# Making the lower halves of the weights' words on ScalarE instead of GpSimd in an attention and Mish feed-forward kernel

## The chip, the core and the metric

The kernel runs on one core of one Trainium2 chip. The metric is the device time of one execution in microseconds; the kernel before was timed three times, and the median counts. A profiled execution of the same program gives the trace.

The core's engines are TensorE (PE in the profile, with its weight loads as PEld), VectorE (DVE), ScalarE (ACT), GpSimd (POOL) and SyncE (SP), which here issues the transfers. Each takes its instructions in the order in which the program lists them for it.

## The reference, cut to what matters

Attention with two kinds of local masks (8 batches, 8 heads, 576 positions, head size 64) is followed by a feed-forward layer with a Mish gate; all in float32:

```python
attn_out = _attn_ref(q, k, v)                      # windowed softmax attention
x = attn_out.transpose(0, 2, 1, 3).reshape(4608, 512)
h = x @ w_in                                       # 512 x 2048
sp = where(h > 20.0, h, log1p(exp(minimum(h, 20.0))))
g = h * tanh(sp)
out = g @ w_out                                    # 2048 x 512
```

The weights w_in and w_out come as arrays of 64-bit words. The host shows the kernel each word as two 32-bit halves, and the kernel makes of the lower half a number from 0 to 7 by a multiplication, an addition and a rounding to int32, which it then puts beneath bits of the upper half.

## The kernel before, in words

The tokens are cut into 16 units of 288 (`u` = 0 to 15, two to a batch). For each unit the kernel loads q, k and v, makes scores, exponentials and values, transposes the result into `x`, multiplies it by w_in (`ff1`, line 790), evicts it through Mish on ScalarE (line 796), forms a gate `g` as two float16 halves, and multiplies by w_out (`ff2`, line 972, in the first three units; `product`, line 933, after).

The weights are read once, ahead of and among the first units. Each of w_in (`k` = 0) and w_out (`k` = 1) is taken in four column groups `g` and two parts `p`, and each part goes through these steps, named `wl`, `wm`, `ww`, `ws` and `wp` with `k.g.p` behind them:

- `wl`: SyncE issues two transfers of 512 KB (line 348 for w_in, line 350 for w_out) into one of four buffers `raw`; group 1 of w_in goes straight to `w2`. A buffer is free again when the `wp` of an earlier part has read it.
- `wm`: the upper halves are scaled into the place of the weights (line 370 on ScalarE for w_in, line 368 on GpSimd for w_out).
- `ww`: three steps. The first makes the lower halves in place (line 411, on GpSimd); the second and third join the bits on VectorE (lines 413 and 415). Part 0.3.0 goes through them in two pieces, so line 411 runs 17 times.
- `ws`: TensorE takes a maximum's ingredient over the joined words (lines 382 and 385), and VectorE makes a scale of it.
- `wp`: the words are split into two float16 halves, on ScalarE (line 422) and VectorE (line 424).

There is no planner at run time: a list `ORDER`, written out in the kernel, names every step, and each time that a name occurs, one more piece of that step (up to its next `yield`) is issued. The instructions of one engine run in the order of the list, and an instruction that waits keeps all that stand behind it on its engine. A number after `=` gives the PSUM bank, of which there are four. The two places of the list that the prediction speaks of most are these (0.2.0's first `ww` is in the first line, 1.2.0's in the last but one):

```python
ff0.7=0 wp0.1.1 ff0.0=1 ww0.2.0 ff0.0 fs0.3 ww0.1.0 ff0.1=2 lv2 ff0.7 ww0.2.1 wp0.1.1 wp0.1.0 ww0.2.1 wl1.1.0 fs0.1
wp0.1.0 ff0.0 pr1 ff0.1 lv2 ff0.7 ff0.6 ff0.1 va1.2=1 wm0.2.0 pr1 va1.2 va1.0=0 va1.0 ld2 va1.0 pr1=3 ld2 ff0.2=2
...
ld3 wl1.2.0 ww1.0.1 ff1.2 ff1.0 ww1.2.0 ff1.6 ff1.7 ww1.0.0 ff1.1=1 ww1.1.0 gt0.1 wp1.1.0 ld3 ff1.5=3 xa2 ff1.1
ff1.1 ww1.0.0 ww1.0.1 tp2.0=2 wp1.1.0 wl1.2.1 tp2.0 ws1.0=1 gt0.2 ws1.0 ff1.5 wp1.0.0 tp2.1=2 ww1.0.1 ff1.2 wp1.0.0
```

An `ff` step has three pieces: two groups of 12 matmuls on TensorE, and the eviction through Mish on ScalarE (`hm`, line 796), which frees the bank. `fs` are small scales on ScalarE (line 769), `va` the values' matmuls (line 689), `sp` the scores' matmuls (line 577, which read `knd`), `tx` the transposes into x (lines 738, 744 and 746), `lv` the loads of v, with a small memset on GpSimd (line 489) ahead of the first of them (line 501).

Of the kernel before, what the change touches and what calls it, by code (L numbers as in the profile page):

```python
# [14 lines left out]
U32 = mybir.dt.uint32  # L15
I64 = mybir.dt.int64
AF = mybir.ActivationFunctionType
ALU = mybir.AluOpType
# [11 lines left out]
LOW_SCALE, LOW_BIAS = 0.9375 * 2.0 ** -29, -2.0 ** -5  # L30
# [157 lines left out]
def attn_mish_ffn_kernel(  # L188
# [11 lines left out]
    nc = tc.nc  # L200
# [154 lines left out]
    def w_dst(k, g, p):  # L355
        c = slice(p * WIDE, (p + 1) * WIDE)
        return w1[g][:, c] if k == 0 else w2[:, g, c]

    def pieces(k, g, p):
        return [slice(c, c + 1) for c in range(WIDE)] if (k, g, p) in BY_BLOCK else [slice(0, WIDE)]  # L360
# [45 lines left out]
    def w_words(k, g, p):  # L406

        lo, hi = raws[k, g, p]
        a = w_dst(k, g, p).rearrange("p c a n -> p c (a n)").bitcast(I32)
        for c in pieces(k, g, p):  # L410
            nc.gpsimd.tensor_scalar(lo[:, c], lo[:, c].bitcast(U32), LOW_SCALE, LOW_BIAS, ALU.mult, ALU.add)
            yield
            nc.vector.scalar_tensor_tensor(a[:, c], a[:, c], 3, lo[:, c], ALU.logical_shift_left, ALU.bitwise_or)
            yield
            nc.vector.scalar_tensor_tensor(lo[:, c], hi[:, c], -0x80000000, a[:, c], ALU.bitwise_and, ALU.bitwise_or)
            yield
# [585 lines left out]
    def keep_warm_short(n):  # L1002
        keep_warm(n, ones_b)


    STEPS = {"ld": loads, "qp": spread_q, "lv": loads_v, "pr": prep, "sp": scores_of_kind, "sc": scores, "tp": transpose_p, "va": values, "tx": transpose_x,
             "ex": exps, "wl": w_load, "wm": w_max, "ws": w_scale, "ww": w_words, "wp": w_split, "fs": ff_scales,
             "ff": ff1, "gt": gate, "fo": ff2, "kw": keep_warm, "kh": keep_warm_short, "ft": top_scale, "rs": rescale,
             "su": w_sums, "so": sums_open, "gq": gate_of, "ga": gate_sums, "fq": product, "mf": masks_first, "cs": constants, "xa": x_alloc, "ol": open_late, "mr": masks_late}
# [52 lines left out]
```

## Time and profile before

| what | us |
|---|---|
| three runs | 858.32, 859.57, 861.2; median 859.57 |
| the profiled execution, its own time | 862.81 |
| span of the profiled execution | 860.9 |
| TensorE busy | 842.1 (98%) |
| VectorE, ScalarE, GpSimd busy | 636.1 (74%), 477.8 (55%), 96.0 (11%) |
| mean granted TensorE clock | 0.992 of full speed |

The span runs from the first to the last instruction that the trace records; 1.9 us of the execution lie around it. Busy time is summed over instructions of an engine. The weights' steps end by 142 us; after that the list holds none of them.

### The profile page before, as it was taken

Reading aid. Unit: us, or ns where it says so; the run is one execution under the profiler, and the core shown is the slowest. Engines: PE = TensorE matmul, PEld = TensorE weight load, DVE = VectorE, ACT = ScalarE, POOL = GpSimd, SP = SyncE. Lnnn points to the kernel's source line nnn. Section 1 sums busy time; section 2 is a strip of 40 time slices with the busy share of each in tenths; the row PEclk is TensorE's granted clock in tenths of the full one; section 3 lists DMA queues with packets and bytes.
Section 4 is the critical chain, followed back from the end, with each engine's and each line's share of the span. In section 5 each row is a group of like instructions: output and inputs, shape, how many; then the busy total and the mean of one; then the engine's idle time right before and its main releaser. Section 6 shows DMA issues by size and latency. Waiting matters only on the chain.

```text
span 860.9 us, 32197 instructions
## 1 busy us (share of the span) xinstructions
PE 842.1 (98%) x14818; PEld 727.3 (84%) x14821; DVE 636.1 (74%) x818; ACT 477.8 (55%) x615; POOL 96.0 (11%) x99
## 2 busy tenths in 40 slices
PE   8798999999999999999999999999999999999998
PEld 7486777788788998988999889988889889988898
DVE  3788998586999897968777587977878764854353
ACT  2464655453486558765753775766446656624342
POOL 5116583210010001000000000010000000000000
PEclk9989999999999999999999999999999999999999
DMA  8648543366320437253623373725335160421001
GB/s 270 213 151 266 154 146 87 73 144 130 70 57 13 126 80 178 57 144 96 126 67 102 69 150 76 131 72 102 94 73 109 43 127 18 57 40 34 1 22 37
DMA packets 154887, 86.29 MB, mean 100 GB/s; under 512 B 92288, under 2 KB 150656, under 8 KB 154752
## 3 DMA queue, kind: packets, MB, share of 16 engines
q1 hardware_dynamic: 154752, 84.24, 40.9%
q8 instruction: 116, 1.90, 1.0%
q14 instruction: 19, 0.16, 0.1%
HBM read 56.89 MB, written 9.44 MB: 77 GB/s over the span
## 4 chain that ended last, share of the span: by engine, by line
PE 86%; DMA 7%; DVE 3%; SPq 2%; ACT 1%; issue 1%; POOL 0%; DVEq 0%; POOLq 0%; ACTq 0%
PE b L790 40%; PE b L933 31%; PE b L972 8%; DMA vf<-in_vd 4%; PE b L689 4%; PE b L577 3%; DMA raw<-in_w_in 2%; DMA knd<-in_kdT 1%; DVE g L903 1%; SPq L348 1%; DVE hm L909 0%; DVE w L424 0%; SPq L501 0%; PE b L385 0%; ACT g L901 0%
## 5 line engine op out<-in xcount | busy, mean ns | idle before, releaser
L790 PE MATMUL b<-x,w 128*128 128x288 f16 x3072 | 393.4, 286 | 0.2 <-ACT hm L796 0.2
L790 PEld LDWEIGHTS <-w 128*128 128x128 f16 x3072 | 295.4, 98 | 75.5 <-issue 0.6
L903 DVE SCALAR_TENSOR_TENSOR g<-hm,sg,g 128x1152 f16<-128x1152 f32 (+1 forms) x104 | 131.3, 1272 | 53.7 <-ACT g L901 52.9
L933 PE MATMUL b<-g,w 128*128 128x144 f16 x2496 | 164.9, 226 | 0.8 <-issue 0.7
L933 PEld LDWEIGHTS <-w 128*128 128x128 f16 x2496 | 158.4, 98 | 3.2 <-issue 1.1
L796 ACT ACTIVATE hm<-b,fs 128x576 f32<-128x576 f32 x128 | 92.8, 738 | 113.5 <-PE b L790 99.2
L901 ACT ACTIVATE g<-hm,sg 128x1152 f16<-128x1152 f32 (+1 forms) x104 | 116.0, 1127 | 40.1 <-PE b L933 26.4
L481 POOL COPY qp<-qn 128x576 f32<-128x576 f32 x15 | 34.9, 2326 | 433.6 <-DMA qn<-in_qT 317.9
L909 DVE TENSOR_TENSOR hm<-hm 128x576 f32<-128x576 f32 x104 | 79.0, 763 | 1.9 <-ACT hm L796 0.4
L972 PE MATMUL b<-g,w 128*128 128x288 f16 x576 | 73.3, 286 | 0.1
L947 ACT ACTIVATE y<-b,fo 128x288 f32<-128x288 f32 x52 | 40.6, 786 | 58.9 <-PE b L933 57.6
L972 PEld LDWEIGHTS <-w 128*128 128x128 f16 x576 | 55.6, 98 | 14.4 <-DVE w L424 0.3
L952 DVE SCALAR_TENSOR_TENSOR y<-b,fo,y 128x144 f32<-128x144 f32 x78 | 33.6, 478 | 45.8 <-PE b L933 22.7
L933 PE MATMUL b<-g,g 128*128 128x144 f16 x936 | 66.6, 226 | 0.3 <-DVE y L952 0.2
L933 PE MATMUL b<-g,late_sums 128*128 128x144 f16 x936 | 65.9, 226 | 0.0
L933 PEld LDWEIGHTS <-g 128*128 128x128 f16 x936 | 60.6, 98 | 2.2 <-issue 0.6
L933 PEld LDWEIGHTS <-late_sums 128*128 128x128 f16 x936 | 60.0, 98 | 0.5
L727 ACT CAST x<-xs 96x512 f16<-96x512 f32 (+1 forms) x39 | 26.7, 686 | 30.9 <-DMA x<-x 17.1
L729 DVE TENSOR_TENSOR x<-xs,x 96x512 f16<-96x512 f32 (+1 forms) x39 | 30.1, 772 | 16.6 <-ACT x L727 16.4
L545 DVE SCALAR_TENSOR_TENSOR vh<-vn,s,vh 128x2688 f16<-128x2688 f32 (+1 forms) x13 | 35.2, 2705 | 8.6 <-ACT vh L543 8.6
L705 DVE TENSOR_TENSOR xs<-b,rec 96x512 f32<-96x512 f32 (+1 forms) x48 | 37.2, 776 | 4.4 <-DVE rec L703 0.5
L689 PEld LDWEIGHTS <-pT 64*32 64x32 f16 (+1 forms) x3276 | 30.2, 90 | 5.3 <-issue 3.6
(127 smaller groups left out, 821.1 us busy)
## 6 DMA issues: line engine op xcount, KB each, us to landing
qn<-in_qT SPq DMA_DIRECT2D x15, 576.0 KB, 5.3
vn<-in_vd SPq DMA_DIRECT2D x66, 128.0 KB, 3.8
raw<-in_w_out SPq DMA_DIRECT2D x16, 512.0 KB, 5.2
out_T<-y SPq DMA_DIRECT2D x26, 288.0 KB, 2.8
raw<-in_w_in SPq DMA_DIRECT2D x12, 512.0 KB, 7.4
vn<-in_v SPq DMA_DIRECT2D x14, 288.0 KB, 4.2
knd<-in_kdT SPq DMA_DIRECT2D x14, 224.0 KB, 4.7
vn<-in_v SPq DMA_DIRECT2D x12, 256.0 KB, 3.7
```

What stands on the lines that cost most here:

```text
L481: nc.gpsimd.tensor_copy(qp.rearrange("p (b r i) -> p b r i", r=NR, i=SQ // NR), d["q"][:, :2 * HT].rearrange("p (b i r) -> p b r i", r=NR, ...
L545: nc.vector.scalar_tensor_tensor(lo, src, s, hi, ALU.mult, ALU.subtract)
L689: nc.tensor.matmul(avv[s * SQ:(s + 1) * SQ, a, t - t0, h * (D + 1):(h + 1) * (D + 1)], p, vv[vi][ks, v0:v0 + D + 1], start=(i == 0), stop= ...
L705: nc.vector.tensor_tensor(xs.rearrange("p (a t h e) -> p a t h e", a=2, h=2, e=D), avv[:, :, :, 1:AW - 1].rearrange("p a t (h e) -> p a t ...
L790: nc.tensor.matmul(ph[:, h, :HT], w1[j][:, c, wi, k * P:(k + 1) * P], x_of(d, xi, c), start=(n == 0), stop=(n == len(seq) - 1))
L796: nc.scalar.activation(d["m"][p][:, half, k0:k0 + 2], ph[:, :, :HT], AF.Mish, scale=d["fs"][:, j:j + 1])
L901: nc.scalar.activation(hi, src, AF.Identity, scale=sg)
L903: nc.vector.scalar_tensor_tensor(lo, src, sg, hi, ALU.mult, ALU.subtract)
L909: nc.vector.tensor_tensor(a, a, b, op=op)
L933: nc.tensor.matmul(acc[e], left(l, e, p, wi)[:, k * P:(k + 1) * P], right(gi, k), start=(n in opens and p == 0 and q == 0), stop=(last and ...
L947: nc.scalar.activation(into(half, t), by(acc), AF.Identity, scale=fo)
L972: nc.tensor.matmul(po[:, :HT], w2[:, e, j, wi, k * P:(k + 1) * P], d["g"][j][:, gi, k, :], start=(j == 0 and n == 0), stop=(j == NCH - 1 a ...
```

## The change

The first `ww` step becomes a ScalarE instruction that computes the same multiplication, addition and rounding, with the same operands and at the same places of the list. GpSimd loses 17 instructions, ScalarE gains 17. All else stays.

```diff
         lo, hi = raws[k, g, p]
         a = w_dst(k, g, p).rearrange("p c a n -> p c (a n)").bitcast(I32)
         for c in pieces(k, g, p):
-            nc.gpsimd.tensor_scalar(lo[:, c], lo[:, c].bitcast(U32), LOW_SCALE, LOW_BIAS, ALU.mult, ALU.add)
+            nc.scalar.activation(lo[:, c], lo[:, c].bitcast(U32), AF.Copy, scale=LOW_SCALE, bias=LOW_BIAS)
             yield
             nc.vector.scalar_tensor_tensor(a[:, c], a[:, c], 3, lo[:, c], ALU.logical_shift_left, ALU.bitwise_or)
             yield
```

## Rows read from the trace of the kernel before

**Rows 1.** The page's busy times of the engines, over the span

```profile
PE 842.1 (98%) x14818; PEld 727.3 (84%) x14821; DVE 636.1 (74%) x818; ACT 477.8 (55%) x615; POOL 96.0 (11%) x99
```

**Rows 2.** Sum of windows from 140 to 860 us, busy time by engine

```profile
sum 720.00, PE 715.92 PEld 627.45 DVE 526.31 ACT 406.82 POOL 28.66; mean PE 19.89 PEld 17.43 DVE 14.62 ACT 11.30 POOL 0.80
```

**Rows 3.** TensorE's waits: line, releaser, total us, times, longest

```profile
PE b L577 <- DMA knd<-in_kdT: 1.8, 2, 1.4
...
PE b L382 <- DVE w L413: 0.9, 1, 0.9
PE b L577 <- DVE x L746: 0.8, 1, 0.8
...
PE b L385 <- DVE w L413: 0.7, 1, 0.7
```

**Rows 4.** Line 411: duration ns min/median/max, and its longest idle's end

```profile
L411 POOL TENSOR_SCALAR raw<-raw x15: 639/1139/1685, 8.3 to 124.8; 128x1024 int32<-128x1024 uint32 x13, 128x512 int32<-128x512 uint32 x2
...
  DMA raw<-in_w_in: 16.4, 4
```

**Rows 5.** ScalarE by line and form, to 140 us: busy, mean ns, idle before

```profile
L422 ACT ACTIVATE w<-raw,ws 128x1024 f16<-128x1024 f32 x14 | 17.3, 1243 | 9.2 <-DVE ws L394 3.7 <-PE b L659 3.6 <-DVE ws L401 1.2
...
L370 ACT ACTIVATE w<-raw 128x1024 f32<-128x1024 f32 x5 | 5.7, 1131 | 17.4 <-DMA raw<-in_w_in 17.4
```

**Rows 6.** ScalarE's timeline around part 0.1.1: start us, us, instruction, idle before

```profile
48.08 0.64 ACT L744 CAST x<-b 128x576 f16<-128x576 f32 x1 [0.41 <-PE b L738]
```

**Rows 7.** ScalarE's timeline around the place of 0.2.0

```profile
57.96 0.30 ACT L769 ACTIVATE fs<-f,f 128x1 f32<-128x1 f32 x1
...
60.87 2.63 ACT L796 ACTIVATE hm<-b,fs 128x576 f32<-128x576 f32 x4
65.42 1.14 ACT L370 ACTIVATE w<-raw 128x1024 f32<-128x1024 f32 x1 [1.92 <-DMA raw<-in_w_in]
```

**Rows 8.** SyncE's timeline, transfers of 0.2.0 and 1.2.0

```profile
59.61 1.08 SPq L348 DMA_DIRECT2D raw<-in_w_in  x2
...
94.47 1.03 SPq L350 DMA_DIRECT2D raw<-in_w_out  x2
```

**Rows 9.** SyncE's waits from 66 to 130 us: total, times, longest

```profile
SPq L501 <- POOL vf L489: 4.2, 1, 4.2
```

**Rows 10.** TensorE's timeline behind the place of 0.2.0

```profile
62.51 1.34 PEld L689 LDWEIGHTS b<-vf,pp 64*32 64x32 f32 x120 [0.24 <-ACT hm L796]
...
77.66 6.97 PE L790 MATMUL b<-x,w 128*128 128x288 f16 x48
```

**Rows 11.** Half-microsecond windows of TensorE: length, busy, granted clock, DMA share, GB/s

```profile
42.00:42.50 0.50, 0.00 (x0) 0.51 0.47 137
42.50:43.00 0.50, 0.02 (x3) 0.50 0.25 73
...
48.50:49.00 0.50, 0.50 (x7) 0.66 0.10 30
...
76.00:76.50 0.50, 0.50 (x56) 0.65 0.89 291
...
79.50:80.00 0.50, 0.50 (x6) 0.94 1.04 315
```

**Rows 12.** Timeline around the place of 1.2.0, four engines

```profile
92.50 1.94 DVE L424 SCALAR_TENSOR_TENSOR w<-raw,ws,w 128x1024 f16<-128x1024 f32 x1 [1.35 <-ACT w L422]
...
98.47 2.00 ACT L796 ACTIVATE hm<-b,fs 128x576 f32<-128x576 f32 x3
99.26 4.57 PE L790 MATMUL b<-x,w 128*128 128x288 f16 x36 [0.22 <-ACT hm L796]
...
102.44 1.50 POOL L411 TENSOR_SCALAR raw<-raw 128x1024 int32<-128x1024 uint32 x1 [9.06 <-DMA raw<-in_w_out]
```

**Rows 13.** VectorE's line 413 beside one of line 411, and undisturbed

```profile
22.71 1.90 DVE L413 SCALAR_TENSOR_TENSOR w<-w,raw 128x1024 int32<-128x1024 int32 x1
...
26.28 1.21 DVE L413 SCALAR_TENSOR_TENSOR w<-w,raw 128x1024 int32<-128x1024 int32 x1
```

## The prediction

> **What bounds the kernel now.** I began with the page's busy times. TensorE works for 842.1 of 860.9 us [rows 1]; the reader should see that it is the bound over the whole, and that a lighter GpSimd (96.0 us) can't matter by its load. The next view is the windows by stage. From 140 us to 860 us TensorE is busy for 715.92 of 720 us [rows 2], so 842.1 - 715.9 = 126.2 us of its work and nearly all its idle time (14 us) lie in the first 140 us, and the weights' steps lie there too. Whatever the first 140 us lose is not won back afterwards: only 4 us of idle time are left there.
>
> The third view is TensorE's waits [rows 3]. Those that bear on the change are 0.9 us and 0.7 us for VectorE's line 413 (the joining of the words), 1.8 us for the transfer of `knd`, and 0.8 us for VectorE's line 746. Then comes line 411 itself [rows 4]. Its instructions last 1.14 us in the middle, and what they mostly wait for is a transfer. That is the point of this case: on GpSimd such a wait costs little, since hardly anything stands behind it. On ScalarE the evictions of the banks stand behind it. So the last views are the timelines of ScalarE, SyncE and TensorE around each place.
>
> **The change, part by part.** *The price of the work.* ScalarE has no instruction of this shape in the trace with an unsigned input and an int32 output. The nearest rows have the same 128x1024 elements and read the same words with a stride: line 370 at 1.131 us, line 422 at 1.243 us [rows 5]. I take 1.13 (both multiply by a constant), with 1.24 as the other end. Seventeen of these are at most 19 us more on ScalarE, which is busy for 477.8 of 860.9 us [rows 1]; the load alone makes no bound. I see no loading of a function table for it: the two lines of rows 5 stand in the same stretch between Exp and Mish without one.
>
> *Fifteen of the seventeen places.* At the places of groups 0.3 and 0.0 ScalarE and GpSimd wait for the same transfer, and ScalarE is ready for it; TensorE is multiplying ones to stay warm there. The pieces of w_out but for 1.2.0 come to a ScalarE whose data has landed, or to one that waits for TensorE anyway. Part 0.1.1 stands between two evictions of `x`, where ScalarE idles 0.41 us ahead of the second [rows 6], which takes up part of the piece; what is left can make the first `ff` late. For all fifteen I take 0.2 us, between 0 and 1.1 us (one piece quite uncovered).
>
> *Place A, part 0.2.0.* In the list its piece stands behind `wp0.1.1` and ahead of `fs0.3`, `wp0.1.0`, `fs0.1` and the four Mish evictions of ff0.0, ff0.7, ff0.6 and ff0.1, and the data is not there yet. SyncE issues the transfer at 59.61 [rows 8], and ScalarE's own line 370 for the same part, which stands behind the evictions, starts at 65.42 when the transfer ends its wait [rows 7]. Now ScalarE waits at this point from about 59 us on, with all four evictions behind it. It goes on at 65.42 + 1.13 = 66.55. From `fs0.3` to the first eviction took 60.87 - 57.96 = 2.91 us, and an eviction takes 2.63 / 4 = 0.66 [rows 7], so bank 1 is free at 66.55 + 2.91 + 0.66 = 70.1. TensorE's next work, `va1.2`, takes bank 1, and started at 62.51 right behind that eviction [rows 10]. The wait is 70.1 - 62.5 = 7.6 us.
>
> What is late next is shortened by this. Between 62.5 and 84.6 TensorE waited 0.9 us for line 413 of this same part, and 1.8 us for `knd` [rows 3]; both are ready when TensorE comes later, so 2.7 us come back. The clock is the other thing. After TensorE's wait that ends just before 43.0, the granted clock is at 0.51, that is 1.2 GHz, from 42.0 until it rises between 48.5 and 49.0 [rows 11]: some 5.6 us of work at half speed behind a wait. After the wait for `knd` it is low from 76.0 to about 79.5 [rows 11]. The new wait is longer than either, so I put 5.6 us of low clock behind it. Streamed matmuls lose half of that, 2.8 us; but the first 2 us are short float32 matmuls of 65 columns, which lose less: 2.3 us, bounds 1.8 and 2.8. The low stretch behind the `knd` wait goes away: 3.5 us, of which 1.84 us are the streamed matmuls from 77.66 on [rows 10], so 0.9 to 1.7 us come back, I take 1.3. Place A: 7.6 - 2.7 + 2.3 - 1.3 = 5.9 us, bounds 5.0 and 6.8.
>
> A gain lies in the same place. SyncE's line 501 waits 4.2 us for GpSimd's memset [rows 9], which stood behind the waiting line 411. GpSimd no longer waits, so SyncE issues what follows (among it `knd`) 4.2 us sooner. But TensorE is late by then, so it is worth nothing beyond the 1.8 us counted above.
>
> *Place B, part 1.2.0.* Its piece stands between the eviction of ff1.0 and those of ff1.6 and ff1.7. The three evictions ran together from 98.47, while GpSimd's line 411 waited 9.06 us for its transfer, till 102.44 [rows 12]. On ScalarE it ends at 102.44 + 1.13, and the eviction of ff1.6, which frees bank 3, at 104.2. TensorE comes to ff1.5, which takes bank 3, after 12 of the 36 matmuls that start at 99.26 in 4.57 us: 99.26 + 1.52 = 100.8 [rows 12]. If place A moves both alike, the wait is 3.4 us. It does so as far as I can follow: SyncE issued this transfer at 94.47 [rows 8], right after VectorE's line 424 ended, 92.50 + 1.94 = 94.44 [rows 12], which frees its buffer, and this hangs on ScalarE's and TensorE's late work. Another low stretch follows a wait of this length; on streamed matmuls with a few transposes I take 2.3 us again (1.8 to 2.8). Place B: 5.7 us. Its bounds are 0, where the transfer lands 3.4 us sooner against TensorE than before, and 7.5, where it lands over a microsecond later.
>
> *What comes back behind it.* The waits of 0.7 us for line 413 and 0.8 us for line 746 [rows 3] lie at 117 and 138 us, where TensorE will be late and VectorE less disturbed. I take 1.0 of the 1.5 us, bounds 0 and 1.5.
>
> *A relief for VectorE.* Line 413 took 1.90 us where a line 411 ran beside it, and 1.21 us alone [rows 13]. The Trainium skill, page "SBUF — State Buffer", section "SBUF: two separate sides", says that VectorE instructions with two SBUF inputs and GpSimd instructions that read SBUF take one port pair in turn, the later one waiting for the other's whole length; the 0.69 us of these rows agrees with that. By that rule the change speeds VectorE at up to 17 places. As a mechanism of this kernel it can shorten only TensorE's waits for VectorE: 0.9 + 0.8 + 0.7 = 2.4 us [rows 3].
>
> *The sum.* 0.2 + 5.9 + 5.7 - 1.0 = 10.8 us. The profiled execution took 862.81 us of its own (its span and 1.9 us around it), so one like it would take 873.6. It stands 3.2 us above the median of the runs, 859.57, on which the sum gives 870.4. I predict 870.
>
> **The rivals.** *Only place A costs.* For it: SyncE is 4.2 us ahead at 63 us, and GpSimd's lighter load can bring 1.2.0's transfer forward against TensorE. Against it: the buffer's release at 94.44 is what the issue waited for. 859.6 + 0.2 + 5.9 - 1.0 = 864.7.
>
> *ScalarE stays behind.* After place B eight or so late pieces could each press on an eviction, at 1.13 us and a further low stretch: 4 to 8 us more, 874 to 878. Against it: ScalarE has waits of its own for TensorE in that stretch.
>
> *No change.* The relief of VectorE is all that counts, because the evictions prove not to wait: 859.6 - 2.4 = 857.2, just inside the 0.3% (2.6 us) that measurement of this kernel can tell from none. The skill's rule above is what speaks for it. Against it is the order of ScalarE's queue.
>
> *Faster.* SyncE's 4.2 us bring `knd` in time, and with the wait of 1.8 us its low clock of 1.3 us goes, and half of the relief besides: 859.6 - 1.8 - 1.3 - 1.2 = 855.3. It decides by one point: at place A the data must be there by 62.5 - 0.66 - 2.91 - 1.13 = 57.8 us, so that no eviction is late. The transfer is issued only at 59.61 [rows 8], behind transfers that wait for neither ScalarE nor GpSimd. So this needs SyncE to be sooner by some 8 us than anything here allows.
>
> **How the numbers follow.** Both places cost: 0.68, at 870, with its own range 865.5 to 874.5 from the bounds of A, B and what comes back, which hardly all fall on one side. Only A: 0.16. ScalarE stays behind: 0.08. No change: 0.04. Faster: 0.04. The range from 864 to 876 leaves out the last two, most of "stays behind" and a part of "only A". Slower: 0.68 + 0.16 + 0.08 = 0.92.
>
> **What would show it.** Right: ScalarE's line 411 starts at about 65.4 with an idle time of some 6 us ahead of it, ended by the transfer of w_in; TensorE waits some 7.6 us for `hm` of line 796 at about 62.5, and its clock falls to 1.2 GHz behind that; the waits for `knd` are gone; a second wait of 3 to 4 us for `hm` stands at about 106; GpSimd's memset no longer holds line 501; from 146 to the end all is as before, about 10 us later. Wrong: the first ScalarE piece of 0.2.0 finds its data landed; or TensorE's second wait is missing (then 864.7); or new waits for line 796 follow behind 120 us. A piece of 1.5 us or more on ScalarE would also spoil the sum.

## The result, and the profile after

The kernel after takes 872.9 us (median of four runs, 869.7 to 874.2), the kernel before 860.4 us (858.3 to 861.8) on the same chip. The ratio is 1.0143, with a 95% interval from 1.012 to 1.0166: 12.3 us slower (10.3 to 14.3; here and below a ratio is turned into us on 860). The prediction said 870 us, from 864 to 876, and slower with 0.92. The profiled execution after took 871.98 us with a span of 870.1, which is 9.2 us above the span of before.

The busy times of the engines in the page of after:

```profile
PE 843.4 (97%) x14821; PEld 727.0 (84%) x14821; DVE 631.4 (73%) x818; ACT 494.4 (57%) x632; POOL 74.1 (9%) x82
```

Beside [rows 1], ScalarE gained 16.6 us and GpSimd lost 21.9; TensorE's own work grew by 1.3 us only. So nearly all of the loss is idle time of TensorE, and its waits in the trace of after say where (line, releaser, total us, times, longest):

```profile
PE b L689 <- ACT hm L796: 7.2, 1, 7.2
PE b L790 <- ACT hm L796: 3.4, 2, 3.3
...
PE b L738 <- DVE xs L705: 1.0, 1, 1.0
...
PE b L577 <- DVE x L746: 0.9, 1, 0.9
...
PE b L577 <- DMA knd<-in_kdT: 0.7, 1, 0.7
```

Two long waits for the Mish evictions of line 796 are new beside [rows 3]. The waits for line 413 are gone, that for `knd` fell from 1.8 to 0.7 us (what is left of it stands near 16 us), and one of 1.0 us for line 705 came.

Line 411 on ScalarE, by its line: durations in ns (least, median, most), then the first and the last start in us:

```profile
L411 ACT ACTIVATE raw<-raw x15: 656/1144/1167, 8.7 to 137.0; 128x1024 int32<-128x1024 uint32 x13, 128x512 int32<-128x512 uint32 x2
```

A piece lasts 1.144 us on ScalarE, as line 370 does [rows 5]. Now ScalarE's timeline around the places of 0.2.0 (first two rows), of 1.1.0 (the third) and of 1.2.0 (the last two): start, duration, instruction, and in brackets the idle time ahead with what ended it.

```profile
63.71 1.14 ACT L411 ACTIVATE raw<-raw 128x1024 int32<-128x1024 uint32 x1 [5.81 <-DMA raw<-in_w_in]
...
67.62 2.63 ACT L796 ACTIVATE hm<-b,fs 128x576 f32<-128x576 f32 x4
...
71.15 1.15 ACT L411 ACTIVATE raw<-raw 128x1024 int32<-128x1024 uint32 x1
...
106.06 1.15 ACT L411 ACTIVATE raw<-raw 128x1024 int32<-128x1024 uint32 x1 [3.13 <-DMA raw<-in_w_out]
107.07 1.38 ACT L796 ACTIVATE hm<-b,fs 128x576 f32<-128x576 f32 x2
```

The four evictions that ran from 60.87 [rows 7] run from 67.62, because the piece ahead of them has waited 5.81 us for its transfer. At the second place the three evictions that ran together [rows 12] are split: one, then a wait of 3.13 us and the piece, then two. TensorE's timeline shows the price:

```profile
49.31 11.92 PE L790 MATMUL b<-x,w 128*128 128x288 f16 x96
...
68.41 2.50 PE L689 MATMUL b<-vf,pp 64*32 64x65 f32 x120 [7.18 <-ACT hm L796]
...
70.89 4.85 PE L790 MATMUL b<-x,w 128*128 128x288 f16 x24
...
82.38 6.10 PE L790 MATMUL b<-x,w 128*128 128x288 f16 x48
...
102.97 1.63 PE L790 MATMUL b<-x,w 128*128 128x288 f16 x12 [0.16 <-ACT hm L796]
107.87 4.77 PE L790 MATMUL b<-x,w 128*128 128x288 f16 x24 [3.27 <-ACT hm L796]
112.48 0.66 PE L659 MATMUL b<-ident,sb 96*128 96x96 f32 x6
...
144.74 0.49 PE L738 MATMUL b<-ident,xs 96*128 96x96 f32 x4
```

The same instructions in the trace of before started at 50.66, 62.51, 63.99, 77.66, 99.26, about 100.8 (worked out, [rows 12]), 103.67 and 135.66. After minus before, TensorE is 1.35 us early at the first of these, 4.7 late at the fourth, 3.7 at 99, 8.8 behind the second wait, 9.1 at 136 and 9.2 at the end. The lead of 1.35 us ahead of place A is scatter between executions: in e4, e10, e11 and e12 below, whose programs up to this point are that of before, this `ff` starts at 48.0 to 50.5 us. So place A cost 4.7 + 1.35 = 6.1 us, of which 1.0 came back by 99 us, which leaves 5.1; place B cost 8.8 - 3.7 = 5.1; and from 146 us on nothing changed.

Windows of 2 us of TensorE behind the first wait (length, busy time, granted clock, DMA share, GB/s):

```profile
62.00:64.00 2.00, 0.00 (x0) 1.00 1.01 411
64.00:66.00 2.00, 0.00 (x0) 0.57 1.06 379
66.00:68.00 2.00, 0.00 (x0) 0.50 1.16 300
...
74.00:76.00 2.00, 2.00 (x14) 0.87 0.03 4
76.00:78.00 2.00, 2.00 (x16) 1.00 0.04 12
```

The granted clock falls to 0.50 (1.2 GHz) while TensorE waits, and rises to 1.00 (2.4 GHz) within the window from 74 us, whose mean is 0.87: at 0.50 for a quarter of it, so till about 74.5. The first 6 us of work, from 68.41 on, run at the lower level.

### The profile page after: what moved, and what is told of

The parts are those of the page before. It is cut to its first block, busy times and chain, and to the rows that moved or that the text cites. A ratio compares the mean times of both kernels' runs of the same rounds, so it can differ in the third digit from the quotient of the medians.

```text
span 870.1 us, 32193 instructions
## 1 busy us (share of the span) xinstructions
PE 843.4 (97%) x14821; PEld 727.0 (84%) x14821; DVE 631.4 (73%) x818; ACT 494.4 (57%) x632; POOL 74.1 (9%) x82
## 4 chain that ended last, share of the span: by engine, by line
PE 86%; DMA 7%; DVE 2%; SPq 2%; ACT 2%; issue 1%; ACTq 0%; DVEq 0%
PE b L790 41%; PE b L933 30%; PE b L972 7%; DMA vf<-in_vd 4%; PE b L689 4%; PE b L577 3%; DMA raw<-in_w_in 2%; DMA raw<-in_w_out 1%; DVE g L903 1%; SPq L348 1%; DVE hm L909 0%; SPq L505 0%; ACT hm L796 0%; PE b L385 0%; ACT g L901 0%
## 5 line engine op out<-in xcount | busy, mean ns | idle before, releaser
L972 PEld LDWEIGHTS <-w 128*128 128x128 f16 x576 | 55.6, 98 | 14.4 <-DVE w L424 0.3
```

Of the source, the lines that this page charges most:

```text
L972: nc.tensor.matmul(po[:, :HT], w2[:, e, j, wi, k * P:(k + 1) * P], d["g"][j][:, gi, k, :], start=(j == 0 and n == 0), stop=(j == NCH - 1 a ...
```

## The experiments

The theory (W): each piece as work costs ScalarE nothing that counts, but at two places, A (0.2.0) and B (1.2.0), it waits for its transfer with evictions behind it. The first rival (L): every piece on ScalarE costs TensorE about alike, 12.3 / 17 = 0.7 us. Ten of the twelve kernels divide the pieces between ScalarE and GpSimd, or move steps; e7 and e9, told further below, add work to TensorE. Times are medians; the kernel before took 859.7 to 860.4 us beside them.

| kernel | on ScalarE | us | ratio to before, 95% | us over before |
|---|---|---|---|---|
| after | all 17 | 872.9 | 1.0143 [1.012, 1.0166] | 12.3 |
| e1 | all but A | 868.7 | 1.0104 [1.0076, 1.0132] | 8.9 |
| e2 | all but B | 866.1 | 1.0073 [1.0049, 1.0096] | 6.3 |
| e3 | all but A and B | 865.0 | 1.0050 [1.0028, 1.0073] | 4.3 |
| e4 | A and B alone | 870.8 | 1.0136 [1.0104, 1.0168] | 11.7 |
| e5 | all but A, B and 1.1.0 | 861.5 | 1.0018 [1.0002, 1.0034] | 1.5 |
| e6 | all 17, three moved in the list | 859.8 | 0.9994 [0.9973, 1.0016] | -0.5 |
| e8 | all but B and 1.1.0, A's load earlier | 862.1 | 1.0029 [1.0015, 1.0042] | 2.5 |
| e10 | 1.1.0 alone | 863.9 | 1.0046 [1.0025, 1.0066] | 4.0 |
| e11 | A alone | 867.1 | 1.0080 [1.0065, 1.0095] | 6.9 |
| e12 | B alone | 861.1 | 1.0019 [1.0006, 1.0033] | 1.6 |

**e1 to e4: A, B, both taken back, and both alone.** All start from the kernel after; the condition is (0,2,0) in e1, (1,2,0) in e2, either of them in e3, and "neither of them" in e4. (With the three lines more, line 796 is line 799 in these kernels, and so on.)

```diff
-            nc.scalar.activation(lo[:, c], ..., AF.Copy, scale=LOW_SCALE, bias=LOW_BIAS)
+            if (k, g, p) in ((0, 2, 0), (1, 2, 0)):
+                nc.gpsimd.tensor_scalar(lo[:, c], ..., LOW_SCALE, LOW_BIAS, ALU.mult, ALU.add)
+            else:
+                nc.scalar.activation(lo[:, c], ..., AF.Copy, scale=LOW_SCALE, bias=LOW_BIAS)
```

> Only the piece of part 0.2.0 goes back to GpSimd; sixteen stay on ScalarE. Theory W (the cost is the wait of ScalarE's queue at two places): TensorE's wait of 7.2 us for the eviction at 61 us is gone, the one of 3.3 us at about 102 us stays; the time falls by the 5.1 us that the two traces show for place A, to 867 to 869, 0.7 to 1.0% above the kernel before. Theory L (each of the seventeen pieces costs ScalarE alike): 12.5 / 17 = 0.7 us less, 872.

> Only the piece of part 1.2.0 goes back to GpSimd. Theory W: the wait of 7.2 us at 61 us stays, the one of 3.3 us at 104 us is gone, and with it 5.1 us: 867 to 869. Theory L: 872, as with any other single piece.

> Both pieces go back to GpSimd; fifteen stay on ScalarE. Theory W: both waits are gone and the time is that of the kernel before, 859 to 862, or up to 1.3 us under it, by what the start of the trace after gained. Theory L: 15 of 17 parts of the cost are left, 871.

> Only the pieces of parts 0.2.0 and 1.2.0 go to ScalarE; fifteen stay on GpSimd. Theory W: nearly the whole cost with 2 of the 17 pieces, 869 to 873, with TensorE's waits of 7 and 3 us for evictions in the trace. Theory L: 2 / 17 of the cost, 862.

e1 and e4 came out within what W expected, e2 0.9 us below it. e4 carries the loss: two pieces of seventeen make 11.7 of 12.3 us, which L (1.4 us) can't give. But e3 is a miss of W: with both places back on GpSimd 4.3 us stay, where the time of the kernel before was expected (859 to 862). TensorE's longest wait in the trace of e3, and the rows of ScalarE that it goes back to:

```profile
PE b L793 <- DVE xs L708: 4.5, 1, 4.5
```

```profile
70.17 1.14 ACT L414 ACTIVATE raw<-raw 128x1024 int32<-128x1024 uint32 x1 [4.63 <-DMA raw<-in_w_out]
71.18 0.59 ACT L700 ACTIVATE den<-b,eps,f 96x8 f32<-96x8 f32 x2
```

There is a third place, C: the piece of 1.1.0 waits 4.63 us for its transfer, and behind it stands `den` of line 700, which VectorE's `xs` needs and TensorE after it. In the kernel after the same piece starts at 71.15 with no wait (the third row of ScalarE's timeline above), since place A has made ScalarE late. One wait hid the other. e1, which has A back too, shows the same wait of TensorE (3.5 us). The theory became W3: three places, of which A covers C.

**e5 and e10: 1.1.0 back as well, and 1.1.0 alone.** The condition for GpSimd is (0,2,0), (1,1,0) or (1,2,0) in e5, and all but (1,1,0) in e10.

> Three pieces go back to GpSimd: 0.2.0, 1.2.0 and 1.1.0; fourteen stay on ScalarE. Theory W3 (three places where ScalarE's queue waits for a transfer; the third, 1.1.0, is covered by the first and shows only when that is gone): the 4.6 us that ScalarE waited at 65.5 us and the 4.5 us that TensorE waited behind it at 68 us are gone, and the time is that of the kernel before, 858 to 861. Theory L' (the 4.9 us left with both pieces back are the price of the fifteen pieces' work on ScalarE): 14 / 15 of it stays, 864 to 865.

> Only the piece of part 1.1.0 goes to ScalarE, sixteen stay on GpSimd. Theory W3: with place A's wait gone ScalarE waits 4 to 5 us for this transfer at 65 to 70 us, with the values' evictions behind it; TensorE waits 3.5 to 4.5 us at 68 us; 863 to 865. Rival: 1.1.0 costs nothing by itself and the 4.9 us came of the fourteen others with it: 860.

Both nearly as W3 says (e5's 861.5 lies just above its range), and e5 not as L' does. The fourteen other pieces on ScalarE cost 1.5 us (0.2 to 2.9), and 1.1.0 alone 4.0 (2.2 to 5.7). Its wait in the trace of e10, on ScalarE and then on TensorE:

```profile
70.53 1.10 ACT L414 ACTIVATE raw<-raw 128x1024 int32<-128x1024 uint32 x1 [4.77 <-DMA raw<-in_w_out]
```

```profile
PE b L793 <- DVE xs L708: 4.7, 1, 4.7
```

**e6: all seventeen on ScalarE, but moved in the list.** 0.2.0's piece goes behind `wm0.2.0`, which waits for the same transfer and has the evictions ahead of it; 1.1.0's goes some two lines down, ahead of `ww1.1.1`; 1.2.0's behind the evictions and matmuls of ff1.6, ff1.7 and ff1.1.

```diff
-... ff0.0=1 ww0.2.0 ff0.0 fs0.3 ...
+... ff0.0=1 ff0.0 fs0.3 ...
-... wm0.2.0 pr1 ...
+... wm0.2.0 ww0.2.0 pr1 ...
-ww1.1.0 pr1 va1.2 ff0.2 ...
+pr1 va1.2 ff0.2 ...
-ww1.1.1 va1.1 sc2.1 ...
+ww1.1.0 ww1.1.1 va1.1 sc2.1 ...
-... ff1.0 ww1.2.0 ff1.6 ff1.7 ... ff1.1 ww1.0.0 ...
+... ff1.0 ff1.6 ff1.7 ... ff1.1 ww1.2.0 ww1.0.0 ...
```

> All seventeen pieces stay on ScalarE, and the list is changed at three places: the first piece of 0.2.0 stands behind the maximum's step of the same part, that of 1.1.0 ahead of that of 1.1.1, that of 1.2.0 behind the eviction of ff1.1; all three find their data landed. Theory W3: none of the waits is left, 856 to 861; the lower end if the transfers that SyncE issues 4 us sooner (GpSimd's memset is no longer held) shorten the wait for knd. Theory L': 864 to 872, since ScalarE does all of the work of the kernel after.

The whole loss is gone, with the same 17 pieces of 1.1 us on ScalarE. Its timeline there:

```profile
65.31 1.13 ACT L370 ACTIVATE w<-raw 128x1024 f32<-128x1024 f32 x1 [1.61 <-DMA raw<-in_w_in]
66.35 1.10 ACT L411 ACTIVATE raw<-raw 128x1024 int32<-128x1024 uint32 x1
...
75.48 1.13 ACT L411 ACTIVATE raw<-raw 128x1024 int32<-128x1024 uint32 x1
...
102.48 1.13 ACT L411 ACTIVATE raw<-raw 128x1024 int32<-128x1024 uint32 x1
```

These are the pieces of 0.2.0, 1.1.0 and 1.2.0, and none of them waits: the first follows line 370, which waited for that transfer in the kernel before too [rows 7]. So it is the place in the queue that costs, not the work. It isn't faster than the kernel before either; no kernel tried here is.

**e8: A's transfer earlier.** `wl0.2.0` is issued two lines sooner in the list, right behind `wl0.2.1`; 1.1.0 and 1.2.0 are on GpSimd, so that A stands by itself. It also tests the rival "faster", which wanted the data at A by 57.8 us.

```diff
-... va0.1 wl0.2.1
+... va0.1 wl0.2.1 wl0.2.0
-... tx0.1 wl0.2.0 ws0.1=2 ...
+... tx0.1 ws0.1=2 ...
```

> Part 0.2.0 stays on ScalarE at its place of the list, but its load is issued right behind that of 0.2.1, some 9 us sooner; 1.1.0 and 1.2.0 are on GpSimd. Theory W3: its data is there by 57.8 us, no eviction is late, TensorE does not wait at 61 us, and the time is that of the kernel before or less, 856 to 861. If the place costs by its work and not by the transfer: as with only place A's cost, 864 to 866.

ScalarE's row of that piece, and TensorE's two behind it:

```profile
58.38 1.17 ACT L414 ACTIVATE raw<-raw 128x1024 int32<-128x1024 uint32 x1 [0.66 <-DMA raw<-in_w_in]
```

```profile
63.15 0.30 PE L692 MATMUL b<-vf,pp 64*32 64x65 f32 x2 [1.63 <-ACT hm L799]
64.19 2.40 PE L692 MATMUL b<-vf,pp 64*32 64x65 f32 x118 [0.74 <-DMA vf<-in_vd]
```

The data is there at 58.4 us, 0.6 us behind the point that the prediction worked out, and TensorE is 1.1 us earlier than in the trace of before (its `ff` starts at 49.60): its wait is 1.6 us in place of 7.2; the transfer of `vf` that was overtaken adds 0.7. The time is 2.5 us over before (1.3 to 3.6), a little more than W3 expected. e5, which has the same pieces on ScalarE but for A, stands at 1.5, and A with its load in the old place (e11) costs 6.9. So A's price follows the landing of that one transfer. No gain appears even so.

**e7 and e9: TensorE kept at work in wait A.** 48 and 24 matmuls of ones (`kw`, line 999) stand in the list ahead of `va1.2`, to separate the wait itself from the low clock behind it.

```diff
-... pr1 ff0.1 lv2 ff0.7 ff0.6 ff0.1 va1.2=1 ...
+... pr1 ff0.1 kw48 lv2 ff0.7 ff0.6 ff0.1 va1.2=1 ...      # kw24 in e9
```

> The kernel after, with 48 multiplications of ones (128x96, some 0.13 us each, 6.4 us) on TensorE ahead of the values of the second unit, in the wait of place A; nothing reads what they make. If the low clock behind the wait is a cost of its own, as the prediction has it (2.3 us): the granted clock stays at full speed from 61 to 75 us, the ff step behind it takes 3.1 us and not 4.9, and the time falls by 2 us, to 871. If it is hidden by what follows: 873, as the kernel after.

> As the run with 48 multiplications of ones in the wait of place A, but with 24 of them; each is two matmuls of 0.11 us, so they last 5.4 us and end before TensorE's wait of 7.2 us does, and bank 3 is free when its eviction comes. If the low clock costs by itself: the clock stays at full speed to 75 us, the ff step behind it takes 3.1 us and the values 1.5, the time falls by 2 to 3 us to 870, unless TensorE waits to be issued its later instructions as it did with 48; those waits are read from the trace and added: 870 and their sum.

Both failed in what they were for. e7 took 893.2 us, ratio 1.0394 [1.0363, 1.0426]; e9 took 903.4, ratio 1.0506 [1.0479, 1.0532]. In e7 a matmul of ones turned out to be two instructions, and the 96 outlast the wait. Its TensorE rows there still measure the clock:

```profile
62.53 10.85 PE L999 MATMUL b<-ones 128*128 128x96 f32 x96
73.31 1.50 PE L689 MATMUL b<-vf,pp 64*32 64x65 f32 x120
74.84 3.10 PE L790 MATMUL b<-x,w 128*128 128x288 f16 x24
```

The same two groups took 2.50 and 4.85 us behind the wait in the kernel after. The low clock of place A costs 1.00 + 1.75 = 2.75 us. In e9 the first group took 1.61 us, at a granted clock of 1.00 too. What made both kernels slower by 20 to 30 us more is another matter, told in the last section.

**e11 and e12: A alone and B alone.** All other pieces on GpSimd.

> Only part 0.2.0 on ScalarE, all other pieces on GpSimd. Theory W3 (three places at which the transfer ends a wait of ScalarE; the first covers that of 1.1.0): one wait of TensorE for the eviction of line 799 of about 7 us near 62 us and none of 3 us near 106; the time is that of the kernel before plus the predicted place A, 5.9 us (5.0 to 6.8). From the pair already measured, both places together are 10.8, so this kernel and the one with 1.2.0 alone should add up to 10.8 within 2 us, since these two waits do not overlap. Rival L (each piece costs alike, about 0.7 us): plus 0.7. Rival, waits that hide one another here too: the single costs add up to well over 10.8.

> Only part 1.2.0 on ScalarE, all other pieces on GpSimd. Theory W3: no wait of TensorE for the eviction near 62 us, one of 2.9 to 3.4 us near 100 us, and a time of plus 5 us over the kernel before (predicted for place B 5.7, with bounds of 0 and 7.5; 10.8 less what part 0.2.0 alone costs). Rival L: plus 0.7. Rival, that B costs only behind a late TensorE: plus 0 to 2, with the transfer landing as late as before against an earlier TensorE or ScalarE still at other work.

A alone costs 6.9 us (5.6 to 8.2), a little above the 5.0 to 6.8 expected; B alone 1.6 (0.5 to 2.8), a miss of W3, which expected 5. Together they make 8.5 and not 10.8. The second rival named B's amount but not the reason: it had the transfer land as late as before. SyncE's timeline and ScalarE's in e12:

```profile
84.35 5.20 SPq L508 DMA_DIRECT2D vf<-in_vd  x2
89.65 0.56 SPq L474 DMA_DIRECT2D knp<-in_kT  x1
94.14 0.92 SPq L350 DMA_DIRECT2D raw<-in_w_out  x2
```

```profile
99.06 1.16 ACT L414 ACTIVATE raw<-raw 128x1024 int32<-128x1024 uint32 x1 [0.18 <-DMA raw<-in_w_out]
```

SyncE's in the kernel after, and VectorE's line 424 there, which frees the buffer of 1.2.0:

```profile
93.06 5.87 SPq L505 DMA_DIRECT2D vf<-in_vd  x2
99.03 0.56 SPq L471 DMA_DIRECT2D knp<-in_kT  x1
99.72 1.07 SPq L350 DMA_DIRECT2D raw<-in_w_out  x2
```

```profile
96.62 1.28 DVE L424 SCALAR_TENSOR_TENSOR w<-raw,ws,w 128x1024 f16<-128x1024 f32 x1 [1.79 <-ACT w L422]
```

SyncE's issue of the same transfer in e11, and its two rows ahead of that in the kernel before:

```profile
100.09 1.07 SPq L350 DMA_DIRECT2D raw<-in_w_out  x2
```

```profile
86.93 6.71 SPq L505 DMA_DIRECT2D vf<-in_vd  x2
93.74 0.56 SPq L471 DMA_DIRECT2D knp<-in_kT  x1
```

In e12 `vf` and `knp` are issued 4.5 us and more ahead of 1.2.0's transfer, which lands 99.06 - 94.14 = 4.9 us after its issue, 0.18 us after ScalarE is ready: no wait. In the kernel after, SyncE is late from place A on (`vf` stands behind transfers that wait for buffers), the three are issued back to back, and 1.2.0's takes 106.06 - 99.72 = 6.3 us, 3.13 us too long. Its buffer is free at 96.62 + 1.28 = 97.9 us, so SyncE's queue and not the buffer holds its issue. In the trace of before it took 102.44 - 94.47 = 8.0 [rows 8, 12], also right behind `vf`, at an earlier ScalarE. So B's wait depends on whether SyncE has run ahead, and in e4, e1 and the kernel after, with A or C ahead of it, it had not (TensorE waits 2.9 to 3.3 us there). That A delays B's transfer is shown by these rows, by that of e11 most plainly: with A alone on ScalarE it is issued at 100.09 us. Why SyncE in e12 issued `knp` some 4 us ahead of the profiled execution of before (89.65 against 93.74) is open, since the two programs are the same up to there; 1.5 us of it lie in the last two issues of `vf` (5.20 against 6.71). The spread of e12's runs (859.2 to 864.1) may hold executions of both kinds; only one of them has a trace.

## Why the prediction was right, point by point

**Right.** The forecast and its sign, and the mechanism: two transfers that ScalarE waits for with evictions behind it. The piece costs 1.144 us (predicted 1.13). At A the wait was 7.18 us (7.6), and its low clock 2.75 (2.3). More came back there than was taken: TensorE was 5.90 + 1.35 = 7.25 us later at the end of the wait, and of 7.25 + 2.75 = 10.0 us 5.1 are left at 99 us, so 4.9 came back (4.0). At B the wait was 3.27 (3.4), and its low clock 1.7 (2.3): 4.77 us for 24 matmuls that take 3.10 at full clock. The two waits for line 413 and most of that for `knd` went, SyncE's line 501 was no longer held, and from 146 us on all is as before. Place A by itself, 5.9 in the sum with bounds of 5.0 and 6.8, measured 6.9 (5.6 to 8.2) alone and 5.1 in the traces; place B, 5.7 in the sum, 5.1 in the traces. A and B together, 11.6 in the sum, measured 11.7 (8.9 to 14.4) in e4. The sum of 10.8 stands beside 12.3 (10.3 to 14.3) measured, and beside 9.2 + 1.35 = 10.55 between the two traces.

**Right by luck: the size of B's wait.** The prediction let the release of the buffer hold back the transfer of 1.2.0. In the kernel after SyncE's queue held it instead, 99.72 - 97.9 = 1.8 us longer, and the transfer then took 6.3 us in place of 8.0, 1.7 less. The two differences cancel.

**Wrong: the fifteen places.** The step "the pieces of w_out but for 1.2.0 come to a ScalarE whose data has landed" is false for 1.1.0 by itself: its piece waits 4.6 to 4.8 us and costs 4.0 alone (e10), more than the bound of 1.1 us for all fifteen. In the kernel after it is true, but only because A comes first; so the sum didn't suffer, which was luck, and the undoing of A and B did. The other fourteen measured 1.5 us (0.2 to 2.9) where 0.2 was taken; e6, which has them on ScalarE too, stands at -0.5 (-2.3 to 1.4), so their price is not sure.

**Wrong: what comes back.** 1.0 us was taken. The wait of 0.7 us for line 413 near 117 us did go, but that for line 746 stayed at 0.9, and the 1.0 us for line 705 came. It is there in the traces of e1, e2, e3, e5, e6 and e8, which have the late pieces on ScalarE, and not in those of e4, e11 and e12, which don't. The piece is that of 1.3.1, which on ScalarE stands among the gates of line 878; VectorE's row behind it in the trace of after:

```profile
138.20 2.36 DVE L413 SCALAR_TENSOR_TENSOR w<-w,raw 128x1024 int32<-128x1024 int32 x2 [2.34 <-issue]
```

In the trace of before the same two ran at 127.93 with no wait. ScalarE made the piece from 136.98 on, VectorE's row starts as it ends, and `xs` comes behind on VectorE. (The profile names no releaser for the wait of 2.34 us; that it is the piece is read from the times.) So behind place B the traces show a loss of 9.1 - 8.8 = 0.3 us and no gain of 1.0. The traces hold this loss already in their 10.55 us; what lies between that and 12.3 is within the interval and stays open.

**Place B's lower bound.** The prediction gave B a bound of 0 "where the transfer lands 3.4 us sooner against TensorE"; that is what e12 shows. B waited in the three traces that have A or C ahead of it. The rival "only place A costs" had that case; A delayed the transfer, and even with B on GpSimd (e2) the time is 866.1 us, not its 864.7.

**The other rivals.** *Faster* hung on data at A by 57.8 us; e8 brought it to 58.4, the wait shrank to 1.6 us, and the kernel stayed 2.5 us slower than before; e6, where A does not wait at all, is not faster either. *No change* by the relief of VectorE: its busy time fell from 636.1 to 631.4 us, and e6, with all seventeen pieces off GpSimd and these waits gone, shows what is left of that in the time: -0.5 us (-2.3 to 1.4). The rule in the Trainium skill, page "SBUF — State Buffer", section "SBUF: two separate sides", that VectorE and GpSimd take a port pair in turn, may hold for single instructions [rows 13], but no gain of it in the time shows here, since TensorE waits little for VectorE. *ScalarE stays behind*: no further wait for line 796 came but one of 0.3 us, which the trace of before has too.

## What to carry to other kernels

An instruction that is moved to another engine takes its wait along: look at what stands behind it in that engine's queue, and whether its data has landed by then, before its busy time; if not, move it in the list too, next to an instruction that waits for the same data anyway (e6: 12 us back). Waits in series hide one another, and an early one can also make a later one by delaying transfers: A, B and C alone cost 6.9, 1.6 and 4.0 us, A and B together 11.7, and all but A and B still 4.3. So take places one at a time and all together before putting a price to each.

## What was not expected of the hardware

With 48 TensorE instructions more near 62 us, TensorE idled hundreds of microseconds later, in what the profile calls "issue": idle time in which the engine waited for nothing that the profile shows. Its rows among TensorE's waits in e9, which has 24 matmuls of ones (48 instructions) more:

```profile
PE b L689 <- issue: 11.7, 5, 4.0
PE b L933 <- issue: 6.7, 6, 1.9
PE b L577 <- issue: 5.4, 3, 2.5
PE b L790 <- issue: 4.2, 3, 3.4
...
PE b L972 <- issue: 2.2, 2, 1.7
```

They sum to 30.2 us, of which 6.7 lie in the first 150 us; the kernel after has 4.8 (lines 689 and 577), all of them there. That is 25.4 of the 33.8 us by which the span of e9's profiled execution (903.9) is longer than that of after. e7, with twice the ones, has 19.9 us of them. The kernels that add no TensorE instruction have at most 7.4 us (the kernel before). Which property of TensorE's instruction stream decides it (how many, or where they fall) stays open; two sizes, of which the smaller is the slower, don't tell.

The other is the clock behind place B. The same 24 matmuls that take 4.77 us in the kernel after, behind a wait of 3.27, have these rows in e4 and in e1:

```profile
107.31 3.10 PE L793 MATMUL b<-x,w 128*128 128x288 f16 x24 [2.86 <-ACT hm L799]
```

```profile
104.65 4.39 PE L793 MATMUL b<-x,w 128*128 128x288 f16 x24 [2.91 <-ACT hm L799]
```

In e4 the granted clock stays at 1.00 in every window of 2 us from 98 to 114; in e1 it falls to 0.50 (1.2 GHz) from 104 on. Behind nearly the same wait the low clock cost nothing in the one and 1.3 us in the other, where the prediction took 2.3.
